# Swapping the operands of k'v in a TensorE-heavy attention and mixing kernel, and packing head pairs in column halves

## The chip, the cores and the metric

The kernel runs on one core of a Trainium2 chip. The metric is the device time in microseconds (us) from the start to the end of one execution; the kernel before was run three times. A profile of one execution stands beside the times. Its span is a little shorter than the time, as it counts from the first to the last recorded instruction.

The engines are TensorE (PE in the profile, its weight loads PEld), VectorE (DVE), ScalarE (ACT), GpSimd (POOL) and SyncE (SP), which here issues the DMAs.

## What is computed

Two blocks follow each other. The first is an attention whose score is a product of two sketches, and so linear in the sequence; the second mixes tokens with a phase (batch 4, heads 4, sequence 1088, head dimension 32, sketch size r = 8, model width 128). Cut to what matters:

```python
def phi(x):
    a = np.einsum('rd,bhsd->bhsr', S1, x)
    b = np.einsum('rd,bhsd->bhsr', S2, x)
    return np.einsum('bhsi,bhsj->bhsij', a, b).reshape(*x.shape[:-1], r * r)
q_p, k_p = (phi(q), phi(k))
kv = np.einsum('bhsf,bhsd->bhfd', k_p, v)         # <- the part that changes
z = np.sum(k_p, axis=2)
num = np.einsum('bhsf,bhfd->bhsd', q_p, kv)
den = np.einsum('bhsf,bhf->bhs', q_p, z)[..., None] + 1e-06
attn = num / den                                   # then (B, S, H*D) = x
theta = x @ w_theta
zr, zi = x * np.cos(theta), x * np.sin(theta)
y = np.einsum('ts,bsd->btd', w_tok_r, zr) + np.einsum('ts,bsd->btd', w_tok_i, zi)
u = x + y
out = u + np.maximum(u @ w_ch, 0.0)
```

`kv` is, for each batch and head, a 64 x 32 matrix: 64 features of a key times 32 values, summed over the sequence. The sequence lies in nine chunks of 128 rows on the partitions.

## The kernel before

The weights come as 64-bit floating point and are turned into fp32 on the chip. For w_tok, which is 34 pieces of 128 x 544, that takes three ScalarE and two VectorE instructions for each piece:

```python
def load_f32(dst, src):
    st = buf("st", [P, PIECE], I64, ST)[:p, :n]
    DMA.dma_start(st, src)
    lo, hi = split(st)
    step = buf("step", [P, NC * P], I16, 3)[:p, :2 * n].rearrange("p (n t) -> p n t", t=2)
    x = dst.bitcast(I32)
    A.activation(dst, hi.bitcast(F32), AF.Copy, scale=2.0**-112)
    A.activation(step[:, :, 1].bitcast(F16), hi.bitcast(F32), AF.Copy, scale=2.0**-60)
    A.activation(step[:, :, 0], lo.bitcast(U32), AF.Copy, scale=2.0**-29)
    ts(x, x, 3, ALU.logical_shift_left)
    tt(V, x, x, step..., ALU.add)
```

For each batch there are stages, named `keys`, `values`, `queries`, `mixed` and `mixing`:

- **keys**: load q, k, v; powers of two to scale by; the sums over keys from which the denominator comes (`ksl`, `cm`, `cz`, `tz`, `nz`, `mv`).
- **values**: transpose k (`big` to `fT`), multiply by the sketches (`s_bd`) to get `ks`, then the features `feat` (VectorE, 128 x 768 for three chunks) and their product with v, accumulated over the nine chunks in one PSUM tile `kv`, and copied into the block-diagonal `kvbd`.
- **queries**: slices of q (`qsl`), their products with `mv` (`lv`), the denominators (`fl`, `dgr`, `dn`, `rd`).
- **mixed**: features of the queries, transposed (`feat` to `fT`), times `kvbd` (`num`); x, its transpose `xT`, theta, cosine and sine; `zr`, `zi` and the last 64 rows of both in `z2`.
- **mixing**: 17 double rows of w_tok (`wT`) against z, in three groups of up to 384 tokens, then the last product with w_ch and the output.

The stage of the values that the change touches, as it was:

```python
    def keys_values(b):
        vn = tiles["v", b]
        kv = psum()[:, :4 * D].rearrange("p (n d) -> p n d", n=2)
        for g in range(NG):                      # 3 groups of 3 chunks
            ks = tiles["kf", b, g]
            kp = buf("feat", [P, CH, R, R], F32, 2)
            tt(V, kp, ks[:, :, 0:R]..., ks[:, :, R:2 * R]..., ALU.mult)
            for i in range(GC):
                for n in range(2):               # two pairs of heads
                    c = g * GC + i
                    T.matmul(
                        kv[:, n], kp[:, i * H + 2 * n:i * H + 2 * n + 2]...,   # weights: 128 columns
                        vn[:, c, 2 * n:2 * n + 2]...,                          # moving: 64 columns
                        start=(c == 0 and n == 0), stop=(c == NC - 1), skip_group_check=True)
        for j in range(2):
            pj = slice(j * R * R, (j + 1) * R * R)
            A.copy(kvbd[b % 2][pj, :, j * D:(j + 1) * D], kv[pj, :, j * D:(j + 1) * D])
```

A pair of heads has 2 x 64 = 128 features and 2 x 32 = 64 values. Of its 128 x 64 product only the two blocks on the diagonal are wanted.

The instructions are not issued in the order of the program text. Every operation is noted first, with a duration by rule and a due time; `lay_out` then places them on each engine: of the operations that could start soonest, the one with the earliest due time. This order is fixed when the kernel is built. The due times follow backward from those of the mixing matmuls, which start at `START[b]`, and are moved by `SOONER` for each stage:

```python
    def dues(self):
        for op in reversed(self.ops):
            for n in op.behind:
                other = self.ops[n]
                other.due = min(other.due, op.due - op.cost - other.late)
        for op in self.ops:
            op.due -= SOONER.get(op.stage, 0)
...
    order.due = START[b] + (PACE * n if len(gs) > 1 else 0.65 * (g * NK + n))
    T.matmul(yp[:, :t1 - t0], z, wT[:, i, t0:t1], start=(n == 0), stop=(n == NK - 1))
```

As all operations are issued from one helper, all have the line L320 in the profile; they are told apart by their tiles.

Of the kernel before, what the change touches and what calls it, by code (L numbers as in the profile page):

```python
# [32 lines left out]
P = 128  # L33
# [3 lines left out]
ROUND = 1.5 * 2.0**23  # L37
TWO_PI = 6.2831850
TINY = 2.0**-60
START = 90, 130, 170, 215  # L40
BIG = 5

SOONER = {"keys1": 20, "keys3": 15, "mixed0": 10, "mixed1": -5, "mixed2": 20, "mixed3": 15,
          "mixing0": -25, "mixing1": -35, "mixing2": -25, "mixing3": -10, "queries0": -5,
          "queries1": -5, "queries2": -10, "queries3": 5, "values0": -5, "values1": 20,
          "values2": 35, "values3": 40}
ST = 6
PACE = 2.5
PIECE = 544
# [64 lines left out]
class Order:  # L114
# [35 lines left out]
    def duration(self, engine, call, out, ins):  # L150

        n = math.prod(out.shape[1:])
        psum = any(isinstance(x, View) and x.buf.tag == "w" for x in ins)
        if engine == "DVE":
            if call == "tensor_reduce":
                n = math.prod(ins[0].shape[1:])
            if call == "reciprocal":
                return 0.29, 0.1
            own = any(isinstance(x, View) and x.shape[1:] == (1,) for x in ins[1:])
            fast = call in ("tensor_scalar", "tensor_copy", "memset") and not psum  # L160
            return 0.09 + n / (1920 if fast and not own else 1400 if fast else 970), 0.1
        if engine == "ACT":
            wide = any(isinstance(x, View) and x.buf.tag == "st" for x in ins)
            own = any(isinstance(x, View) and x.shape[1:] == (1,) for x in ins[1:])
            return 0.05 + 0.07 * own + n / (900 if out.dtype != F32 and wide else 1020 if wide else 1130), 0.15
        if engine == "SP":
            return 0.36, 0.0
        if call == "transpose":
            return 0.11, 0.3
        if ins[0].dtype == F32:  # L170
            return max(0.22, n / 600), 0.3
        return max(0.06, n / 2400), 0.3

    def note(self, engine, fn, call, a, kw):
# [30 lines left out]
    def dues(self):  # L205
# [4 lines left out]
        for op in self.ops:  # L210
            op.due -= SOONER.get(op.stage, 0)

# [111 lines left out]
def kernel(  # L324
# [12 lines left out]
    B, _, NC, H, D = q.shape  # L337
# [14 lines left out]
    V, A, T, DMA = order.dve, order.act, order.pe, order.sp  # L352

    def buf(tag, shape, dt=F32, bufs=1):
        return order.buffer(sb, tag, shape, dt, bufs)

    def psum():
        return order.buffer(ps, "w", [P, 512], F32, 8)

    def tt(eng, o, a, b, op):  # L360
        eng.tensor_tensor(out=o, in0=a, in1=b, op=op)
# [72 lines left out]
    ident = buf("ident", [P, P], F32)  # L434
# [16 lines left out]
    t_ = psum()  # L451
    T.transpose(t_[:2 * H, :P], View(hm.buf, hm.buf.slots[0]), ident)
    A.activation(hmT, t_[:2 * H, :P], AF.Copy, scale=512.0)
    hmTq = buf("hmTq", [P, P])[:H]
    t_ = psum()
    T.transpose(t_[:H, :P], hm, ident)
    A.activation(hmTq, t_[:H, :P], AF.Copy, scale=512.0)
# [81 lines left out]
    kvbd = []  # L539
    for b in range(2):  # L540
        t = buf(f"kvbd{b}", [P, 2, 2 * D], F32)
# [137 lines left out]
    def keys_values(b):  # L679

        vn = tiles["v", b]
        kv = psum()[:, :4 * D].rearrange("p (n d) -> p n d", n=2)
        for g in range(NG):
            ks = tiles["kf", b, g]
            kp = buf("feat", [P, CH, R, R], F32, 2)
            tt(V, kp, ks[:, :, 0:R].unsqueeze(3).to_broadcast([P, CH, R, R]),
               ks[:, :, R:2 * R].unsqueeze(2).to_broadcast([P, CH, R, R]), ALU.mult)
            for i in range(GC):
                for n in range(2):
                    c = g * GC + i  # L690
                    T.matmul(
                        kv[:, n], kp[:, i * H + 2 * n:i * H + 2 * n + 2].rearrange("p h i j -> p (h i j)"),
                        vn[:, c, 2 * n:2 * n + 2].rearrange("p h d -> p (h d)"),
                        start=(c == 0 and n == 0), stop=(c == NC - 1), skip_group_check=True)
        for j in range(2):
            pj = slice(j * R * R, (j + 1) * R * R)
            A.copy(kvbd[b % 2][pj, :, j * D:(j + 1) * D], kv[pj, :, j * D:(j + 1) * D])


    NT = NC * HR  # L700
# [145 lines left out]
    def mix_sums(b, gs, yps):  # L846
        zr, zi, zl = tiles["z", b]
        for n, i in enumerate(rows):
            z = zr[:, i] if i < NF else zi[:, i - NF] if i < NK - 1 else zl
            for g, yp in zip(gs, yps):  # L850
                t0, t1 = g * GC * P, min((g + 1) * GC * P, S)
                order.due = START[b] + (PACE * n if len(gs) > 1 else 0.65 * (g * NK + n))
                T.matmul(yp[:, :t1 - t0], z, wT[:, i, t0:t1], start=(n == 0), stop=(n == NK - 1))
# [40 lines left out]
    n = 2 * R  # L894
# [29 lines left out]
    for i in range(NL):  # L924
        T.matmul(pp[:, i * D:], s2x[:, i].rearrange("p h d -> p (h d)"), s2z[:, 0:NL - i],
                         start=(i == 0), stop=(i == NL - 1), skip_group_check=True)
# [21 lines left out]
    for b in range(B):  # L948
        if b:
            order.stage = f"keys{b}"  # L950
            load(b, "kqv")
            powers_of(b)
            order.stage = f"keys{b}"
            keys_slices(b)
        matrices(b)
        order.stage = f"values{b}"
        keys_features(b)
        keys_values(b)
        order.stage = f"queries{b}"
        query_slices(b)  # L960
        features(b)
        denominators(b, 0, NC)
        order.stage = f"mixed{b}"
        for g in range(NG):
            mixed(b, g, numerator(b, g))
        if b == 0:
            order.stage = "weights"
            for i in rows:
                for n in range(0, S, PIECE):
                    load_f32(wT[:, i, n:n + PIECE], w_tok[i][:, n:n + PIECE])  # L970
        order.stage = f"mixing{b}"
        mixing(b)
# [44 lines left out]
```

## Time and profile before

| | before |
|---|---|
| time, median of 3 | 297.95 us (297.94 to 299.46) |
| span of the profile | 296.2 us |
| TensorE busy, instructions recorded | 257.5 us (87%), 1347 |
| TensorE weight loads busy | 185.4 us (63%) |
| VectorE busy | 225.9 us (76%) |
| ScalarE busy | 165.3 us (56%) |
| mean granted TensorE clock | 0.928 |
| matmuls of the mixing stage (128 x 384 and 128 x 320) | 132.5 us in 384 records |
| matmuls of k'v | 19.3 us in 144 records |

A busy share is an average over the whole span. What an operation is worth depends on the stage in which it lies, so the shares are read slice by slice and not as totals. An fp32 matmul leaves two records, each with a weight load of its own. The length of a record is not what it costs when others follow at once: for that, take the distance from one start to the next.

### The profile page before, as it was taken

The numbers are of one execution on the slowest core, as the hardware profiler recorded it, in microseconds if no ns is written. First come the engines' busy times: TensorE is split into PE (matmuls) and PEld (weight loads), VectorE is DVE, ScalarE is ACT, GpSimd is POOL, SyncE is SP. The second block draws the span as 40 slices with busy tenths as digits, with TensorE's granted clock in tenths as the row PEclk, the third lists the DMA queues.
The fourth block names the chain that finished last, engine by engine and source line by source line (L and its number), as shares of the span: only waits on it lengthen the run. The fifth ranks groups of instructions, "written<-read, shape, count | busy, mean of one in ns | idle before, by whom it ended". The sixth has DMA issues, their size and how long they took to land.

```text
span 296.2 us, 4006 instructions
## 1 busy us (share of the span) xinstructions
PE 257.5 (87%) x1347; PEld 185.4 (63%) x1347; DVE 225.9 (76%) x646; ACT 165.3 (56%) x334; POOL 0.7 (0%) x6
## 2 busy tenths in 40 slices
PE   4569558837989999489999999999999999999993
PEld 3447437636966666257876676687758766665671
DVE  4999999999869999999998878999699561001011
ACT  3695559895299999999947225037914360000000
POOL 0000000000000000000000000000000000000000
PEclk9958859995599999979999999999999999999998
DMA  7970559671023757764000000000100000000001
GB/s 258 412 298 2 180 185 321 200 212 52 2 75 85 244 207 240 257 195 143 0 1 2 0 27 27 3 1 14 36 27 2 0 22 27 2 27 22 27 0 49
DMA packets 11603, 28.77 MB, mean 97 GB/s; under 512 B 1216, under 2 KB 5568, under 8 KB 11584
## 3 DMA queue, kind: packets, MB, share of 16 engines
q1 hardware_dynamic: 11584, 28.53, 28.7%
q8 instruction: 10, 0.16, 0.2%
q14 instruction: 9, 0.07, 0.1%
HBM read 26.30 MB, written 2.23 MB: 96 GB/s over the span
## 4 chain that ended last, share of the span: by engine, by line
PE 69%; DVE 15%; ACT 11%; DMA 3%; issue 1%; ACTq 0%; DVEq 0%
PE w L320 69%; ACT step L320 5%; DVE big L320 2%; DVE feat L320 2%; DVE lv L320 2%; DMA st<-w_tok 2%; DVE wT L320 1%; ACT wT L320 1%; ACT big L320 1%; DMA big<-k_l 1%; ACT lv L320 1%; DVE ksl L320 1%; DVE cut_r L320 1%; DVE m L320 1%; DVE fl L320 1%
## 5 line engine op out<-in xcount | busy, mean ns | idle before, releaser
L320 PE MATMUL w<-wT,st 128*128 128x384 f32 (+1 forms) x384 | 132.5, 476 | 1.9 <-DVE st L320 1.3
L320 PEld LDWEIGHTS w<-wT,st 128*128 128x128 f32 x384 | 67.7, 191 | 34.9 <-DVE st L320 2.2
L320 ACT ACTIVATE step<-st 128x544 f16<-128x544 f32 (+2 forms) x70 | 53.1, 808 | 1.8 <-DVE wT L320 1.7
L320 ACT COPY fT<-w 128x256 f32<-128x256 f32 (+1 forms) x48 | 18.5, 399 | 33.1 <-PE w L320 31.4
L320 ACT COPY ot<-w 128x384 f32<-128x384 f32 (+2 forms) x16 | 6.0, 395 | 47.8 <-PE w L320 47.7
L320 PE MATMUL w<-ident,feat 128*128 128x128 f32 x72 | 17.4, 311 | 9.5 <-ACT fT L320 6.1
L320 DVE SCALAR_TENSOR_TENSOR uT<-w,uT 128x384 f32<-128x384 f32 (+1 forms) x12 | 6.4, 532 | 25.2 <-PE w L320 25.1
L320 PEld LDWEIGHTS w<-kvbd,fT 128*128 128x128 f32 x144 | 23.5, 226 | 3.0 <-ACT fT L320 0.9
L320 DVE CUSTOM_DVE_ANT_0 wT<-wT,step 128x1088 uint16<-128x1088 uint16 x34 | 23.8, 717 | 0.3 <-ACT step L320 0.3
L320 PE MATMUL w<-kvbd,fT 128*128 128x64 f32 x144 | 24.0, 296 | 0.0
L320 PE MATMUL w<-big,feat 128*128 128x64 f32 x144 | 19.3, 276 | 5.0 <-DVE feat L320 5.0
L320 ACT ACTIVATE wT<-st 128x544 f32<-128x544 f32 x34 | 22.9, 696 | 1.0 <-DMA st<-w_tok 1.0
L320 PEld LDWEIGHTS w<-big,feat 128*128 128x128 f32 x144 | 18.2, 194 | 7.5 <-DVE feat L320 6.3
L320 PEld LDWEIGHTS w<-ident,feat 128*128 128x128 f32 x72 | 11.6, 179 | 12.0 <-ACT fT L320 7.1
L320 PE MATMUL w<-mv,qsl 128*128 128x192 f16 (+2 forms) x108 | 17.4, 286 | 1.8 <-DVE mv L320 1.6
L320 DVE TENSOR_TENSOR uT<-xT,w 128x384 f32<-128x384 f32 (+1 forms) x12 | 6.3, 528 | 16.2 <-PE w L320 16.2
L320 ACT COPY lv<-w 128x384 f32<-128x384 f32 x36 | 16.0, 483 | 3.7 <-PE w L320 3.7
L320 PE MATMUL w<-ident,big 128*128 128x128 f32 x72 | 13.9, 333 | 3.1 <-DMA big<-k_l 3.1
L320 PE MATMUL w<-s_bd,fT 128*128 128x64 f32 x72 | 11.8, 313 | 5.4 <-DVE pw L320 3.9
L320 PEld LDWEIGHTS <-qsl 128*128 128x128 f16 x108 | 10.6, 102 | 8.4 <-issue 4.2
L320 PE MATMUL w<-ksl 128*128 128x384 f16 x72 | 14.9, 360 | 0.9 <-ACT big L320 0.9
L320 PEld LDWEIGHTS w<-s_bd,fT 128*128 128x128 f32 x72 | 10.6, 223 | 6.6 <-DVE pw L320 4.2
(187 smaller groups left out, 412.7 us busy)
## 6 DMA issues: line engine op xcount, KB each, us to landing
st<-w_tok SPq DMA_DIRECT2D x34, 544.0 KB, 4.6
big<-k_l SPq DMA_DIRECT2D x4, 576.0 KB, 4.0
big<-q_l SPq DMA_DIRECT2D x4, 576.0 KB, 3.9
big<-v_l SPq DMA_DIRECT2D x4, 576.0 KB, 5.2
out<-ot SPq DMA_DIRECT2D x8, 192.0 KB, 2.1
out<-ot SPq DMA_DIRECT2D x4, 128.0 KB, 1.8
st<-w_sq SPq DMA_DIRECT2D x1, 256.0 KB, 3.8
out<-ot SPq DMA_DIRECT2D x4, 32.0 KB, 1.8
```

Source lines behind the costliest of these rows:

```text
L320: op.call(*r, **{k: x.real() if isinstance(x, View) else x for k, x in op.kw.items()})
```

## The change

The values become the weights and the features the moving operand: 64 weight columns in place of 128, 128 moving columns in place of 64. The product is then transposed (64 values by 128 features), and each of the two pairs of heads gets a half of TensorE's columns and of PSUM's partitions (`tile_position=(0, 0)` and `(0, 64)`), so that the two could run beside each other. At the end of each batch ScalarE copies the sum to SBUF, TensorE transposes it, and the copies into `kvbd` read the transposed tile. The rule for durations halves the cost of a matmul with at most 64 weight columns, and the due times of the stages are set anew. A small buffer (`hmTq`) shares the place of the new one.

```diff
--- before.py
+++ after.py
@@ -37,13 +37,13 @@
 ROUND = 1.5 * 2.0**23
 TWO_PI = 6.2831850
 TINY = 2.0**-60
-START = 90, 130, 170, 215
+START = 95, 130, 170, 215
 BIG = 5
 
-SOONER = {"keys1": 20, "keys3": 15, "mixed0": 10, "mixed1": -5, "mixed2": 20, "mixed3": 15,
-          "mixing0": -25, "mixing1": -35, "mixing2": -25, "mixing3": -10, "queries0": -5,
-          "queries1": -5, "queries2": -10, "queries3": 5, "values0": -5, "values1": 20,
-          "values2": 35, "values3": 40}
+SOONER = {"keys1": 20, "keys3": 10, "mixed0": 10, "mixed1": 15, "mixed2": 20, "mixing0": -25,
+          "mixing1": -35, "mixing2": -15, "mixing3": -10, "queries0": -25, "queries1": -5,
+          "queries2": -10, "queries3": -5, "values0": -5, "values1": 10, "values2": 15,
+          "values3": 35}
 ST = 6
 PACE = 2.5
 PIECE = 544
@@ -168,7 +168,7 @@
         if call == "transpose":
             return 0.11, 0.3
         if ins[0].dtype == F32:
-            return max(0.22, n / 600), 0.3
+            return max(0.22, n / 600) / (1 if ins[0].shape[1] > 64 else 2), 0.3
         return max(0.06, n / 2400), 0.3
 
     def note(self, engine, fn, call, a, kw):
@@ -451,7 +451,7 @@
     t_ = psum()
     T.transpose(t_[:2 * H, :P], View(hm.buf, hm.buf.slots[0]), ident)
     A.activation(hmT, t_[:2 * H, :P], AF.Copy, scale=512.0)
-    hmTq = buf("hmTq", [P, P])[:H]
+    hmTq = buf("kvt", [P, P])[:H]
     t_ = psum()
     T.transpose(t_[:H, :P], hm, ident)
     A.activation(hmTq, t_[:H, :P], AF.Copy, scale=512.0)
@@ -679,7 +679,7 @@
     def keys_values(b):
 
         vn = tiles["v", b]
-        kv = psum()[:, :4 * D].rearrange("p (n d) -> p n d", n=2)
+        kv = psum()[:, :P]
         for g in range(NG):
             ks = tiles["kf", b, g]
             kp = buf("feat", [P, CH, R, R], F32, 2)
@@ -688,13 +688,18 @@
             for i in range(GC):
                 for n in range(2):
                     c = g * GC + i
-                    T.matmul(
-                        kv[:, n], kp[:, i * H + 2 * n:i * H + 2 * n + 2].rearrange("p h i j -> p (h i j)"),
-                        vn[:, c, 2 * n:2 * n + 2].rearrange("p h d -> p (h d)"),
-                        start=(c == 0 and n == 0), stop=(c == NC - 1), skip_group_check=True)
+
+                    T.matmul(kv[n * 2 * D:(n + 1) * 2 * D], vn[:, c, 2 * n:2 * n + 2].rearrange("p h d -> p (h d)"),
+                             kp[:, i * H + 2 * n:i * H + 2 * n + 2].rearrange("p h i j -> p (h i j)"),
+                             start=(c == 0), stop=(c == NC - 1), tile_position=(0, n * 2 * D), skip_group_check=True)
+        kvt = buf("kvt", [P, P])
+        A.copy(kvt, kv)
+        t = psum()[:, :P]
+        T.transpose(t, kvt, ident)
+        t = t.rearrange("p (n d) -> p n d", n=2)
         for j in range(2):
             pj = slice(j * R * R, (j + 1) * R * R)
-            A.copy(kvbd[b % 2][pj, :, j * D:(j + 1) * D], kv[pj, :, j * D:(j + 1) * D])
+            A.copy(kvbd[b % 2][pj, :, j * D:(j + 1) * D], t[pj, :, j * D:(j + 1) * D])
 
 
     NT = NC * HR
```

## Prediction

> **What bounds the kernel now.** I read the page first, its forty slices before its totals, then the busy time by stretch, then the order of time on TensorE. In the slices (one is 7.4 us) the question is which row is full at the same time as which stage.
>
> ```profile
> PE   4569558837989999489999999999999999999993
> DVE  4999999999869999999998878999699561001011
> ACT  3695559895299999999947225037914360000000
> PEclk9958859995599999979999999999999999999998
> ```
>
> VectorE is full from slice 2 to slice 21, TensorE from slice 18 to the end, ScalarE in between, and TensorE's clock is low now and then before slice 12. So there are two stages: a first one that VectorE and ScalarE set (they turn the 17 double rows of w_tok into fp32 beside the work of batches 0 and 1), and a second one that only TensorE sets. To place the border I asked for the end of the w_tok conversion on VectorE, and for busy times on either side of it (columns: stretch, length, then busy us of PE, PEld, DVE, ACT, POOL).
>
> ```profile
> 146.13 0.72 DVE L320 CUSTOM_DVE_ANT_0 wT<-wT,step 128x1088 uint16<-128x1088 uint16 x1
> ...
> 0.00:60.00 60.00, 40.55 (x260) 31.62 (x260) 54.84 (x215) 41.22 (x81) 0.70 (x6) 0.83 0.64 234
> 60.00:90.00 30.00, 22.26 (x125) 19.93 (x126) 26.27 (x82) 21.18 (x47) 0.00 (x0) 0.72 0.26 76
> 90.00:130.00 40.00, 34.71 (x166) 23.25 (x165) 39.56 (x70) 39.06 (x71) 0.00 (x0) 0.96 0.65 214
> 130.00:146.10 16.10, 14.95 (x90) 10.86 (x90) 15.84 (x33) 15.47 (x30) 0.00 (x0) 0.99 0.31 98
> 146.10:296.20 150.10, 145.07 (x711) 99.77 (x709) 89.43 (x250) 48.35 (x111) 0.00 (x0) 0.99 0.06 16
> ```
>
> Up to 146.1 us VectorE is busy for 54.84 + 26.27 + 39.56 + 15.84 = 136.5 us, so only 9.6 us of it are idle; TensorE is idle for 146.1 - 112.5 = 33.6 us. After it TensorE works for 145.07 of 150.10 us, and most of the missing 5 us is the last output's way. The chain of waits agrees: from 138.4 to 289.9 us it is TensorE alone. A saving on TensorE counts in full in the second stage and hardly at all in the first.
>
> What the operation itself costs I read from the order of time on TensorE (start, length, tiles, number of records).
>
> ```profile
> 157.93 1.45 PE L320 MATMUL w<-big,feat 128*128 128x64 f32 x12
> 159.21 5.38 PE L320 MATMUL w<-wT,st 128*128 128x384 f32 x16
> 164.43 0.24 PE L320 MATMUL w<-tz,pbd 128*128 128x32 f16 x4
> ```
>
> Every fp32 matmul leaves two records: k'v is 4 batches x 9 chunks x 2 pairs = 72 instructions, and the page counts 144. Twelve records of k'v from 157.93 to 159.21 are 107 ns each; sixteen mixing records from 159.21 to 164.43 are 326 ns each, 0.85 ns a column. At that rate 64 moving columns would be 54 ns, so k'v does not wait for its moving operand. [...]
>
> ```profile
> L320 PE MATMUL w<-big,feat 128*128 128x64 f32 x144 | 19.3, 276 | 5.0 <-DVE feat L320 5.0
> L320 PEld LDWEIGHTS w<-big,feat 128*128 128x128 f32 x144 | 18.2, 194 | 7.5 <-DVE feat L320 6.3
> ```
>
> A record is 276 ns long but starts every 107 ns; the difference, some 170 ns, is pipeline that the next one hides.
>
> [...]
>
> **The change part by part.** *The matmuls.* Swapped, a record has 64 weight columns[...] and 128 moving columns. A 128 x 128 fp32 transpose, with as many moving columns, starts every 110 ns in this trace. So the swap alone gains nothing: 107 becomes 110. All depends on the second half of the columns running beside the first; then two records take 110 ns, 55 each. All 144: 144 x 107 = 15.4 us becomes 7.9, a saving of 7.5. By stages: batches 0 and 1 have their k'v before 60 us and batch 2 between 108 and 126, where TensorE has gaps; only batch 3 (36 records from 157.9 to 172.9) is in the second stage: 36 x 52 = 1.9 us.
>
> *What is added.* A ScalarE copy of 128 x 128 (about 0.3 us by the one activation of that shape) and a transpose (two records, 0.22 us) for each batch, and one more hop ahead of kvbd. In the second stage: 0.2 us of TensorE. I chose to leave the longer hop out, since other TensorE work fills it there.
>
> *Mode changes.* By the order of the changed kernel the 72 instructions stand in 5, 10, 4 and 4 runs for batches 0 to 3, other matmuls between them. Each run is entered and left: 46 changes, 8 of them in the second stage. At no more than 0.17 us that is up to 1.4 us there, so the matmuls by themselves are worth 1.9 - 0.2 - (0 to 1.4) = 0.3 to 1.7 us at the end.
>
> *The due times.* These move more. I laid both orders beside each other and took as the border the first mixing matmul of batch 0's last row, which needs the last w_tok row. Behind it the changed kernel has 18 k'v instead of 18 (1.9 us less), 6 fewer of each of the num, x-transpose and theta matmuls (18 x 0.217 = 3.9 us less), 2 fewer wide mixing ones (1.3), three small ones fewer (0.2) and three other transposes or so more (0.5): some 6.6 us of TensorE less by such rates, 147.0 against 153.6. Before, the 153.6 took 296.2 - 146.3 = 149.9 us, a ratio of 0.976, so the changed second stage should take 147.0 x 0.976 = 143.5 us.
> That work has not vanished; it is ahead of the border, and there VectorE pays. Up to and with its last w_tok conversion its instructions sum by the mean durations of their rows to 171.7 us against 164.6. Means overlap (all its rows sum to 267.6, the page has 225.9 busy), so 7.1 becomes 7.1 x 0.844 = 6.0 us more. If VectorE keeps its 9.6 us of idle time, the border moves from 146.3 to 152.3 and the end to 295.8 us. If half the idle time goes (batch 1 is begun sooner, which gives VectorE something to do where it had waited), the border is at 147.5. The dues were set anew for the new order, so I take two thirds of the way between the two, 149.1, which is a choice and no measurement. With 143.5 us behind it and 0.8 us for mode changes the profile ends at 293.4 us. The measured time is 297.95 - 296.2 = 1.75 us more than the span: **295.1 us**.
>
> **The rivals.** (A) The halves do not overlap. Then k'v stays at 110 ns a record, the second stage is 1.9 us longer and the mode changes are pure loss: 297 to 298.5. [...] I give this 30%. (B) The border just moves: VectorE's extra 6.0 us delay the last w_tok row and eat the shorter second stage; about 297.5. For it: VectorE at 39.56 of 40 us from 90 to 130. (C) The retuned dues also remove the low clock between 60 and 90 us (0.72) and VectorE's gaps, so the border stays at 147 to 148: 147.5 + 143.5 + 1.75 = 292.7, and below 292 if the tail has no mode cost. [...]
>
> **Range and chances.** The end is the sum of two numbers that I know to about 2 us each: the border (147 to 153) and the rest (142 to 146). That gives 290.5 to 298.5 us. 2% faster is below 292.0, which needs (C) together with overlapping halves: 0.17. 2% slower is above 303.9; nothing above gets there save a wait in the second stage that I don't see: 0.03.
>
> **What would show it.** In the changed profile: the k'v records under the reversed names, 144 of them, with starts 55 ns apart inside a run (right) or 110 (rival A); a gap of 0.1 to 0.2 us at either end of a run (mode change) or none; four transposes of kvt; the last w_tok conversion on VectorE near 150 us (147 for C, 152 for B); TensorE full behind it and about 143 us long. If TensorE shows idle time behind the border that waits for kvbd or feat, the prediction is wrong for a reason not listed; if the end moves by more than 2% with the border and the rest both as before, the reading of two stages is wrong.

## The result and the profile after

The changed kernel takes **303.19 us** (median; 303.04 to 303.81) beside 298.22 us for the kernel before on the same chip: a ratio of 1.016, with a 95% interval of 1.013 to 1.020. Ratios, here and below, leave out executions more than 1.5% above the shortest of the same kernel, which the medians keep. It is slower by 5 us. The prediction was 295.1 us with a range up to 298.5, so it was wrong. The span of the profile is 301.1 us (before 296.2), the mean granted TensorE clock 0.905 (0.928).

The forty slices of the changed kernel, one 7.5 us:

```profile
PE   4659592870598889999999999999999999999993
DVE  5998979979996999999999966998851995600011
ACT  4693559799963999888973225327614135500000
PEclk9959867596555899999999999999999999999998
```

Counted from 1, TensorE has a hole in slices 10 and 11 (0 and 5), where the kernel before has 7 and 9 and a smaller hole of its own in slice 9 (3); the clock is low in slices 11 to 13; and from slice 16 on TensorE is full, where it was full to the end only from slice 19 before. Next the busy time by stretch (columns: stretch, length, busy us of PE, PEld, DVE, ACT and POOL, then the clock, the DMA share and GB/s). The first two stretches end and begin at the border, the first mixing matmul of batch 0's last row; the last one is the stretch before the border in which TensorE has no gap:

```profile
0.00:155.90 155.90, 119.29 (x678) 86.59 (x678) 141.50 (x416) 123.07 (x240) 0.70 (x6) 0.82 0.48 170
155.90:301.10 145.20, 140.21 (x676) 93.17 (x674) 85.37 (x231) 43.80 (x98) 0.00 (x0) 0.99 0.06 16
70.00:80.00 10.00, 1.19 (x6) 1.06 (x6) 10.00 (x17) 10.00 (x18) 0.00 (x0) 0.50 0.54 200
80.00:90.00 10.00, 10.00 (x48) 9.07 (x47) 9.62 (x29) 7.06 (x17) 0.00 (x0) 0.50 0.66 228
90.00:100.00 10.00, 8.88 (x37) 6.47 (x38) 7.10 (x28) 4.80 (x11) 0.00 (x0) 0.50 0.25 82
...
107.00:156.00 49.00, 49.00 (x269) 34.18 (x268) 47.20 (x97) 46.13 (x91) 0.00 (x0) 1.00 0.38 127
```

The same view of the kernel before, for the stretches that differ most:

```profile
70.00:80.00 10.00, 9.68 (x49) 9.04 (x49) 8.97 (x29) 3.12 (x8) 0.00 (x0) 0.50 0.01 2
80.00:90.00 10.00, 8.66 (x53) 7.17 (x52) 7.62 (x27) 9.15 (x19) 0.00 (x0) 0.87 0.19 57
90.00:100.00 10.00, 10.00 (x44) 6.29 (x43) 10.00 (x14) 10.00 (x18) 0.00 (x0) 1.00 0.50 155
...
107.00:156.00 49.00, 42.56 (x238) 30.82 (x238) 48.33 (x104) 42.39 (x79) 0.00 (x0) 0.97 0.44 147
```

The border in the order of time on TensorE, before and after:

```profile
146.31 0.81 PE L320 MATMUL w<-wT,z 128*128 128x384 f32 x2
```

```profile
155.86 0.86 PE L320 MATMUL w<-wT,z 128*128 128x384 f32 x2
```

It went from 146.3 to 155.9 us (+9.6), and what lies behind it from 149.9 to 145.2 us (-4.7). That is the whole of the +4.9 us. Ahead of the border VectorE is busy for 141.5 us (136.7 before) and idle for 14.4 (9.6).

TensorE's side tells more. I cut the span into stretches of 2 us and split each in three: idle (length less busy), lost to the low clock (busy times one less the clock), and the rest, work at full clock. The split is an estimate from two spacings: twelve `num` records from 85.33 to 87.94 us take 218 ns each at clock 0.50, and eight in the kernel before, from 147.31 to 148.23, take 115 ns each at 1.00.

| TensorE, us | idle | lost to low clock | work at full clock | span |
|---|---|---|---|---|
| before, to 108 us | 27.2 | 13.7 | 67.1 | |
| before, behind it | 11.5 | 1.6 | 175.2 | 296.2 |
| after, to 108 us | 36.6 | 18.3 | 53.0 | |
| after, behind it | 5.0 | 0.0 | 188.2 | 301.1 |

At 108 us the changed kernel is 14.1 us of TensorE work behind (9.4 more idle, 4.6 more at low clock). It wins back 8.1 us because TensorE has no more gaps afterwards, and 1.1 us because its work is less; some 4.9 us stay. Over the whole span that is 2.9 us more idle time, 3.0 us more at low clock and 1.1 us less work. What a us at low clock is worth can't be read from this pair alone: the profile of the kernel before is one of its executions with a high mean clock (0.928), most have 0.904 to 0.917, and on one chip 297.93 us at 0.928 stands beside 297.95 us at 0.908.

Where the 14 us went is seen in the order of time on TensorE (start, length, tiles, records, and in brackets the idle time before it and who ended it):

```profile
61.16 0.34 PE L320 MATMUL w<-mv,qsl 128*128 128x384 f16 x1
61.42 0.43 PE L320 MATMUL w<-feat,big 128*64 128x128 f32 x2
61.79 0.30 PE L320 MATMUL w<-mv,qsl 128*128 128x288 f16 x1
...
65.05 0.55 PE L320 MATMUL w<-ident,big 128*128 128x128 f32 x3
78.81 1.30 PE L320 MATMUL w<-ident,feat 128*128 128x128 f32 x5 [13.21 <-DVE feat L320]
```

TensorE waits 13.2 us for the first features of batch 0's queries (5.6 before, from 62.7 to 68.3, where ScalarE's copy `fT` came last). VectorE, ahead of these features:

```profile
67.91 0.72 DVE L320 CUSTOM_DVE_ANT_0 wT<-wT,step 128x1088 uint16<-128x1088 uint16 x1
...
69.21 0.71 DVE L320 CUSTOM_DVE_ANT_0 wT<-wT,step 128x1088 uint16<-128x1088 uint16 x1
...
74.62 1.35 DVE L320 CUSTOM_DVE_ANT_0 wT<-wT,step 128x1088 uint16<-128x1088 uint16 x2
...
77.72 1.82 DVE L320 TENSOR_TENSOR feat<-fl 128x768 f32<-128x768 f32 x2
```

The new due times put w_tok pieces (six last conversions from 60 to 78 us; the kernel before has none between 60.4 and 80) in front of the features, which begin at 77.7 us instead of 67.2. Of these 10.5 us, 5.7 are there already when `fl`, from which they are made, begins (66.94 instead of 61.22). The rest comes between `fl` and the features: some 3.3 us of w_tok pieces, and some 2 us of slicing (`step` and `big`) that the kernel before has behind its features. ScalarE is as full there: 10.00 of 10 us from 70 to 80. After the wait TensorE has clock 0.50 until 100 us, through ten us in which it is busy without a gap (10.00 of 10 from 80 to 90).

### The profile page after: what moved, and what is told of

It reads as the page before. It is cut to its first block, busy times and chain, and to the rows that moved or that the text cites. A ratio compares the mean times of both kernels' runs of the same rounds, so it can differ in the third digit from the quotient of the medians.

```text
span 301.1 us, 4002 instructions
## 1 busy us (share of the span) xinstructions
PE 259.5 (86%) x1351; PEld 179.8 (60%) x1351; DVE 226.9 (75%) x646; ACT 166.9 (55%) x338; POOL 0.7 (0%) x6
## 4 chain that ended last, share of the span: by engine, by line
PE 78%; DVE 13%; ACT 3%; DMA 3%; issue 2%; ACTq 0%; DVEq 0%
PE w L320 78%; DMA big<-k_l 3%; DVE big L320 2%; DVE wT L320 2%; ACT step L320 1%; DVE m L320 1%; DVE cut_r L320 1%; ACT big L320 1%; DVE feat L320 1%; DVE fl L320 1%; DVE cut_z L320 1%; ACT lv L320 0%; DVE mx L320 0%; DVE ksl L320 0%; DVE lv L320 0%
## 5 line engine op out<-in xcount | busy, mean ns | idle before, releaser
L320 PE MATMUL w<-wT,st 128*128 128x384 f32 (+1 forms) x384 | 130.9, 473 | 0.0
L320 ACT COPY fT<-w 128x256 f32<-128x256 f32 (+1 forms) x48 | 18.3, 397 | 25.9 <-PE w L320 22.4
L320 PE MATMUL w<-mv,qsl 128*128 128x192 f16 (+2 forms) x108 | 21.9, 324 | 8.2 <-DVE mv L320 6.0
L320 PE MATMUL w<-ident,feat 128*128 128x128 f32 x72 | 15.3, 312 | 13.2 <-DVE feat L320 13.2
L320 ACT COPY lv<-w 128x384 f32<-128x384 f32 x36 | 16.7, 485 | 17.3 <-PE w L320 17.0
L320 PE MATMUL w<-s_bd,fT 128*128 128x64 f32 x72 | 13.3, 318 | 4.8 <-DVE pw L320 4.4
L320 PEld LDWEIGHTS w<-s_bd,fT 128*128 128x128 f32 x72 | 11.3, 224 | 6.9 <-DVE pw L320 4.6
L320 PE MATMUL w<-feat,big 128*64 128x128 f32 x144 | 15.4, 295 | 0.0
L320 DVE TENSOR_SCALAR wT<-wT 128x544 int32<-128x544 int32 x34 | 14.4, 432 | 0.0
L320 PEld LDWEIGHTS w<-ident,big 128*128 128x128 f32 x72 | 11.1, 178 | 4.7 <-DMA big<-k_l 3.2
```

Source lines behind the costliest of these rows:

```text
L320: op.call(*r, **{k: x.real() if isinstance(x, View) else x for k, x in op.kw.items()})
```

## The experiments

Most kernels here keep the **order of one kernel on every engine** and change only what is issued at a place in it. Four that were laid out anew told little, as will be seen; they stand behind those with filler. Each ratio is to the kernel before on the same chip, with its 95% interval.

**New order, old k'v.** Laid out as the changed kernel; in the places of k'v the old form is issued, and the transpose is left out.

```diff
-  T.matmul(kv[half n], vn[..n..], kp[..n..], tile_position=(0, n * 2 * D), ...)
-  A.copy(kvt, kv); T.transpose(t, kvt, ident); A.copy(kvbd.., t..) twice
+  nc.tensor.matmul(kvo[:, n], kp[..n..], vn[..n..], ...)   # same places in the order
+  nc.scalar.copy(kvbd.., kvo..) twice                      # in the place of the first copy
```

> The changed kernel's order of instructions on every engine, kept as it is, but k'v in its old form (128 weight columns, no copy and transpose at the end). Theory D (the new due times lose the time: batch 0's query features come at 77.7 us in place of 67.2, TensorE waits 13.2 us for them and is at half clock from 70 to 100 us; the swapped k'v itself is worth 0 to 2 us): 303 to 306 us, no better than the changed kernel. Rival K (the swapped k'v itself is slow, by mode changes and the longer hop to kvbd): 297 to 300 us.

Measured 303.58 us, ratio 1.016 (1.012 to 1.019); border 156.2, rest 145.6. The wait for the query features is there too:

```profile
77.69 1.30 PE L323 MATMUL w<-ident,feat 128*128 128x128 f32 x5 [12.77 <-ACT step L323]
```

So **the order of the changed kernel, which its due times and durations make, loses the 5 us by itself**; the new form of k'v in it is worth 0.4 us, which the intervals don't tell from nothing.

**Old order, new k'v.** The reverse: the order of the kernel before, the new form in the places of the old, the transpose three TensorE instructions later.

```diff
-  T.matmul(kv[:, n], kp[..n..], vn[..n..], ...)
+  nc.tensor.matmul(kvn[half n], vn[..n..], kp[..n..], tile_position=(0, n * 2 * D), ...)
+  nc.scalar.copy(kvt, kvn); transpose after 3 more TensorE operations; copies after 1 more of ScalarE
```

> The order of the kernel before, kept as it is, but k'v in its new form in two column halves, with the copy, the transpose (a few TensorE instructions later) and the copies into kvbd. Theory D: 296 to 298.5 us, at or a little below the kernel before. Rival K: 301 to 304 us, most of the loss is there.

301.30 us, 1.009 (1.006 to 1.013); border 149.0, rest 150.6. The new form costs about 2.6 us in the old order, so there rival K is right. Two differences show in the trace, neither tested by itself. The stretch in which mv and k'v of batches 0 and 1 alternate takes 8.4 us (53.30 to 61.68) instead of 6.5 (52.95 to 59.41); but the granted clock was 0.64 from 54 to 56 us and 0.51 from 56 to 58, where it was 1.00 before, and that alone is 1.7 us of work by the split used above (2.00 x 0.36 + 2.00 x 0.49). And kvbd of batch 3 now ends a wait of 0.5 us on TensorE at 177 us.

**Both pairs in one half.** The changed kernel; both pairs use the first 64 columns and partitions.

```diff
-  kv[n * 2 * D:(n + 1) * 2 * D] ... tile_position=(0, n * 2 * D)
+  kvo[:, n]                                                     # kvo: 64 partitions, 2 x 128
```

> The changed kernel's order, operands swapped, but both pairs of heads in the first half of the columns (PSUM partitions 0 to 63, one pair behind the other), then two half copies by ScalarE in place of one. If the halves run beside each other in the changed kernel (its k'v records start 67 ns apart in a run): 107 to 112 ns here, and 1 to 3 us longer than the changed kernel, 304 to 306 us. If they do not: 67 ns here as well and 303 us. If the column tiles cost by mode changes more than they bring: below 303 us.

308.82 us, 1.032 (1.027 to 1.037), longer than the forecast. The order of time on TensorE, this kernel and then the changed one:

```profile
170.94 1.52 PE L702 MATMUL w<-feat,big 128*64 128x128 f32 x12
172.40 0.91 PE L323 MATMUL w<-uT,w 128*128 128x384 f32 x2
```

```profile
28.96 0.88 PE L320 MATMUL w<-feat,big 128*64 128x128 f32 x12
29.77 0.43 PE L320 MATMUL w<-s_bd,fT 128*128 128x64 f32 x2
```

Twelve records in one half take 1.46 us from start to start, 122 ns each; in two halves 0.81 us, **67 ns**. So the halves do overlap, 1.8 times and not twice.

**Grouped, new order.** The changed kernel's order; the six k'v instructions of a group are held until the last is due and issued together, which leaves 12 runs.

```diff
+  op.emit = hold(op) until 2 * GC are held, then issue all six
```

> The changed kernel's order, the six k'v instructions of a group of chunks together at the place of the last. Mode changes as the cost: batch 1's ten runs become three, 1 to 2 us less ahead of the first query features: 301.5 to 302.8 us. VectorE's own chain sets that stage: 303 to 303.5 us.

301.76 us, 1.010 (1.006 to 1.013): 1.4 us less than the changed kernel. Work at full clock falls from 241.2 to 237.1 us, idle time grows from 41.6 to 42.9. Standing alone so cost the k'v instructions 4 us of TensorE and, by the medians, 1.4 of the time; the intervals of the two kernels still touch.

**Grouped, old order.** The same in the order of the kernel before.

> As the run with the order of the kernel before and k'v in its new form, but the six k'v instructions of a group of chunks stand together at the place of the last of them: 12 runs or fewer in place of one run for each place where other matmuls came between. If the changes of tiling are what the new form costs there (about 0.25 us for an instruction that stands alone, about 10 of them ahead of the border): the border comes back from 149.0 to 147 us or less and the time is 298 to 299.5 us, as the kernel before. If the changes cost nothing and the longer hop to kvbd does: 301 to 301.5 us as ungrouped.

301.80 us, 1.011 (1.007 to 1.015); border 148.4. That is close to the second forecast, though the changes of tiling do cost something: the query features are back at 67.3 us and work at full clock falls from 242.3 to 238.4. In this pair of profiles 5.8 us more go to the low clock (21.1 against 15.3). The twelve theta records of this kernel, then of the kernel before:

```profile
82.92 2.18 PE L335 MATMUL w<-w,xT 128*128 128x128 f32 x12
84.94 0.27 PE L335 MATMUL w<-ident,feat 128*128 128x128 f32 x1
```

```profile
82.73 1.56 PE L320 MATMUL w<-w,xT 128*128 128x128 f32 x12
84.12 0.27 PE L320 MATMUL w<-ident,feat 128*128 128x128 f32 x1
```

The same work takes 2.02 us instead of 1.39 there; the clock was 0.50 from 82 to 84 us and 0.94 from 84 to 86, where the kernel before had 0.84 and 1.00.

**Filler in the wait, new order.** The changed kernel with 28 dummy fp32 matmuls of 128 x 256 in the 13 us wait.

```diff
+  for _ in range(28): nc.tensor.matmul(tr[:, :2 * P], ident, w2, ...)   # ahead of batch 0's first query transpose
```

> The changed kernel with 28 more fp32 matmuls of 128x256 (about 12 us at full clock), whose output is written over, ahead of batch 0's first query transpose, where TensorE waited 13.2 us. They keep TensorE busy through the wait. Theory: the low clock behind the wait is what costs (18 us of TensorE work at half speed from 80 to 100 us, with VectorE waiting for it 3 to 5 us): clock near 1.0 from 80 us on and 297 to 300 us. Rival: VectorE alone sets the stage, and the clock costs nothing: 302.5 to 304 us.

302.12 us, 1.011 (1.007 to 1.016); border 153.9. TensorE is busy for 12.00 of 12 us from 66 to 78, at clock 1.00. By stretch:

```profile
70.00:80.00 10.00, 8.92 (x44) 7.38 (x42) 10.00 (x19) 10.00 (x16) 0.00 (x0) 1.00 0.51 192
80.00:90.00 10.00, 7.49 (x51) 6.43 (x51) 9.94 (x29) 7.72 (x19) 0.00 (x0) 0.87 0.68 236
90.00:100.00 10.00, 8.24 (x42) 5.32 (x42) 8.93 (x33) 6.28 (x14) 0.00 (x0) 0.67 0.31 93
```

The clock is up, though not wholly (0.67 from 90 to 100). What is lost to it ahead of 108 us falls from 18.3 to 13.9 us, as in the kernel before (13.7). The border comes 2.0 us sooner, the time 1.1, and both forecasts missed. By this run most of the loss is not the clock's; the last run with filler, below, leaves a doubt.

**Filler elsewhere.** Five more kernels ask what the clock costs in the other orders, and in the new order with k'v grouped. Two of them put the filler (12 matmuls) into the PSUM buffer of the first query transpose:

> The kernel before with 12 more fp32 matmuls of 128x256 (about 5.2 us), whose output is written over, in the 5.6 us in which TensorE waits for the first query features. Theory that the low clock behind that wait (0.50 from 70 to 80 us) costs here as it did in the changed kernel (where filling gave 1.1 us): clock 0.9 or more from 70 to 80 us and 296 to 297.8 us, below the kernel before. If the clock is free here because VectorE is full: 298 to 299 us.

> Grouped k'v in its new form in the order of the kernel before, and the 12 filling matmuls as well. If the effects add: the grouped run's time less what filling gives the kernel before, so 295.5 to 298 us, below both kernels. If the new form has no gain in the second stage either: as the filled kernel before or a little above.

300.79 us (1.009, 1.005 to 1.013) and 305.16 us (1.019, 1.013 to 1.025): the filler stood behind that buffer and so the transpose came only at 74.3 and 76.1 us. They test nothing but that. The next two wrote to columns of an earlier buffer that nobody reads (24 matmuls of 128 x 128):

> The kernel before with 24 more fp32 matmuls of 128x128 (5.2 us) in the 5.6 us wait for the first query features, this time into unused columns of a PSUM buffer that nobody reads before 130 us, so they start at once. Clock theory: first query transpose at 68.3 us as before, clock 0.9 to 1.0 from 70 to 80 us in place of 0.50, TensorE's work of 68 to 87 us done some 5 us sooner, and VectorE's waits of 0.8 and 2.0 us behind it gone: 295.5 to 297.5 us. If VectorE's instructions alone set that stage: 298 to 299 us.

> Old order, k'v in its new form and grouped, and the same 24 matmuls in the same wait. If the 3 us that the grouped run lost to the kernel before were lost clock: level with the filled kernel before or up to 1 us below it, 295 to 297.5 us. If they are the longer hop to kvbd and VectorE: 2 to 3 us above the filled kernel before.

The kernel before with it: 298.18 us, ratio 0.9998 (0.998 to 1.002). Grouped k'v in the old order with it: 300.97 us, 1.009 (1.006 to 1.012), border 148.2 and rest 151.0 against 147.2 and 150.0. From 70 to 80 us the clock was 0.64 in the first (0.50 without filler, forecast 0.9 to 1.0) and 0.78 in the second (0.50 in the grouped run without filler). So the part of the low clock that the filler took away, 1.9 us of work in the first (9.68 x 0.50 less 8.13 x 0.36), is worth nothing in the kernel before; the whole was not tested. In the old order the new k'v still loses its 2.8 us with less low clock.

> The changed kernel's order with k'v grouped and the 28 filling matmuls in its 13.2 us wait. Each alone took 1.1 and 1.4 us off the changed kernel's 303.2. If they add: 300 to 301.2 us, still above the kernel before, since VectorE's 4.8 us of work moved ahead of the last w_tok row remain. If only one of them can act: 301.5 to 302.2 us.

Grouped k'v and the 28 filler matmuls in the new order: 301.76 us, 1.005 (1.001 to 1.008). By the median of twenty executions that is no less than grouping alone, and the border in the profile is at 154.8 us in both. The lower ratio says little, since it counts only the shortest seven of the twenty. But two of these took 297.13 and 298.61 us, and they are the two with the highest mean clock, 0.948 and 0.946; the others have 0.917 to 0.931. The profile is of one of the others: there the filler held the clock only from 70 to 80 us (1.00) and not from 80 to 90 (0.55). So in this order a clock that stays up may be worth 3 to 4.6 us, nearly the whole loss. That is two executions without a trace, and no test.

**Laid out anew.** Four kernels change due times or the form of k'v and let the order follow.

```diff
 e1: the changed kernel with START and SOONER of the kernel before
 e2: the kernel before with START and SOONER of the changed kernel
 e4: the changed kernel,  -"queries0": -25  +"queries0": -5
 e7: the kernel before,   +"weights": 5
```

> The changed kernel with START and SOONER as in the kernel before; the order is laid out anew. Border theory (the end is VectorE's work up to the last w_tok conversion, plus its idle time, plus TensorE's work behind): by the orders VectorE has 137.9 us before the border and TensorE 146.1 us behind it (149.7 x 0.976), so a span of 284.1 + 7 to 13 us of idle time = 291 to 297 and a time of 293 to 299 us. Theory that the swapped k'v costs some 2.6 us wherever it stands: 300 to 302 us.

> The kernel before with START and SOONER of the changed one; the order is laid out anew. Border theory: VectorE 138.2 us before the border, TensorE 155.5 behind it, so a span of 293.7 + 7 to 13 = 301 to 307 and a time of 302 to 308 us: the new due times lose with the old k'v too. Rival (the loss comes only with both together): 297 to 300 us.

> The changed kernel with one due time as before: batch 0's queries 20 us sooner (queries0 -5 in place of -25); the order is laid out anew. Border theory: VectorE 142.7 us before the border, TensorE 144.8 behind it: 287.5, and with idle time as in the kernel before (7 us) to as in the changed one (13 us) a span of 294.5 to 300.5 and a time of 296 to 302 us; TensorE's wait for the first query features should shrink from 13.2 us to under 6 us. If the late queries of batch 0 are not the cause: 303 us and the long wait stays.

> The kernel before with the w_tok stage due 5 us sooner than its dates said; the order is laid out anew. The last conversion then has only 108.0 us of VectorE's work ahead of it and TensorE 170.7 us behind its border: 278.7 + 7 to 13 = 286 to 292 and a time of 288 to 294 us, if the end is still VectorE's part plus TensorE's part. If batch 0's z and not w_tok holds TensorE then, TensorE waits behind the border and it is 298 us or more.

308.94 (1.035, 1.033 to 1.038), 307.33 (1.028, 1.025 to 1.032), 307.46 (1.027, 1.020 to 1.034) and 352.38 us (1.180, 1.177 to 1.184); e2 came as expected. In e7 the second forecast did (298 us or more, with TensorE waiting behind the border: 12.7 of the first 50.2 us there are idle, though the longest waits are for `feat` and `cz` and not for z). e1 and e4 met neither of theirs; in e4 the wait for the first query features shrank only from 13.2 to 10.9 us, and its four executions lie between 304.40 and 312.22. Due times are not terms of a sum: one number of the table moves the whole order. In e7, where the w_tok stage is due 5 us sooner, TensorE keeps clock 0.51 from 60 to 110 us and the rest is 201.7 us long. The table also shows what the new due times are for: with the old ones the swapped k'v costs 10.6 us (308.94 against 298.36), with the new ones 5; and either form of k'v with the table of the other comes to 307 to 309.

**VectorE's work taken away.** Three kernels (h1, h2 and h3, in this order) leave out the two VectorE instructions (0.42 + 0.72 us) of five w_tok pieces, 5.7 us in all, so those pieces are not those of the reference; the order is kept.

```diff
+  if seen[m] - 1 in LEAVE: continue      # shift and add of the 7th to 11th piece (h1), 22nd to 26th (h2, h3)
```

> The order of the changed kernel, kept; the two VectorE instructions of five w_tok pieces (the 7th to 11th in VectorE's order, between 60 and 76 us) are left out, so these pieces of w_tok are not those of the reference. That is 5 x 1.14 = 5.7 us less VectorE ahead of batch 0's first query features, which were ready at 77.7 us. If the time is lost because TensorE stands still behind VectorE at 65 to 79 us, its wait of 13.2 us shrinks by 3 to 5.7 us, the border comes from 155.9 to 150.5 to 153 and the time from 303.2 to 297.5 to 300.5. If ScalarE (10.0 of 10 us busy from 70 to 80) or the clock sets it all the same: the wait stays above 11 us, time 302 to 303.5.

302.44 us, 1.010 (1.005 to 1.016); span 300.4, border 155.4. TensorE's order of time:

```profile
76.56 1.30 PE L327 MATMUL w<-ident,feat 128*128 128x128 f32 x5 [10.69 <-DVE feat L327]
...
78.97 0.19 PE L327 MATMUL w<-tz,pbd 128*128 128x32 f16 x1 [1.10 <-ACT ks L327]
79.61 1.54 PE L327 MATMUL w<-kvbd,fT 128*128 128x64 f32 x6 [0.46 <-ACT fT L327]
```

The features come 2.25 us sooner (75.47 on VectorE), but two waits on ScalarE (1.6 us) take their place, ScalarE being busy for 10.00 us from 70 to 80 as before; 0.5 us reach the border. So neither forecast came whole: the wait shrank by 2.5 us, to below 11, and the time is that of the second one.

> The order of the changed kernel, kept; the same two VectorE instructions are left out for five pieces of w_tok that stand between 115 and 137 us, so these pieces are not those of the reference. Again 5.7 us less VectorE ahead of the border. If VectorE's work sets the border, as the prediction had it, the border comes from 155.9 to 150 to 151.5 and the time from 303.2 to 298 to 299. If TensorE, which has no gap from 107 us on, sets the border by its own queue, the border stays at 155 or later and the time at 302.3 to 303.5.

302.59 us, 1.011 (1.006 to 1.016); span 301.4, border 156.2. One stretch of it:

```profile
107.00:156.00 49.00, 48.86 (x267) 33.98 (x267) 43.34 (x87) 46.53 (x92) 0.00 (x0) 1.00 0.38 127
```

VectorE has 3.9 us less work there than in the changed kernel, TensorE is full all the same, and the border has not moved forward. **In the changed kernel VectorE's work does not set the border; TensorE's own queue does.**

> The order of the kernel before, kept; the two VectorE instructions of five w_tok pieces that stand between 113 and 127 us are left out, so these pieces are not those of the reference. If VectorE's work sets the border there, as the prediction read it, the border comes from 146.3 to 140.5 to 142.5 and the time from 298.2 to 292.5 to 294.5. If TensorE's own queue sets it there too, only the few waits of TensorE on VectorE between 107 and 138 us go (1.3 us by the order of time), and the time is 296.5 to 298.5.

298.70 us, ratio 1.001 (0.998 to 1.004). The stretch ahead of the border in this kernel, and in the kernel before:

```profile
107.00:146.00 39.00, 32.94 (x172) 23.58 (x171) 33.77 (x60) 36.87 (x67) 0.00 (x0) 0.87 0.55 186
```

```profile
107.00:146.00 39.00, 32.56 (x179) 23.44 (x179) 38.71 (x72) 37.42 (x68) 0.00 (x0) 0.96 0.55 184
```

The border is at 147.5 us (146.3 in the kernel before), so five us less of VectorE bring nothing even there. Two things stand beside it: ScalarE is as full (37 of 39 us) as VectorE had been, and the clock was lower in this profile, 0.87 against 0.96, which is 3 us of work (32.94 x 0.13 less 32.56 x 0.04). The clock doesn't hide a gain in the times, though: the executions have mean clocks of 0.906 to 0.922, and those of the kernel before on that chip 0.900 to 0.927. What holds the border there I did not separate.

## Why the prediction was wrong, point by point

- **Halves overlap: right, the size off.** 67 ns a record, not 55, where transposes with as many moving columns take 110 and both pairs in one half 122; rival A was false. What sets the 107 ns of the old form, no run here separates.
- **Mode changes: right in size, and counted in the wrong place.** The mixing group of 16 behind a k'v run takes 5.32 us in the old order with the new k'v (161.51 to 166.83), where it took 5.22. These 0.10 us are within the 0.17 us of the prediction, which was an estimate: the 276 ns of a record less the 107 ns from start to start. But an instruction that stands alone between others takes 0.37 us (61.42 to 61.79 above), where the old form in the same order took 0.20, both at clock 1.00:

```profile
60.38 0.36 PE L702 MATMUL w<-big,feat 128*128 128x64 f32 x2
60.58 0.33 PE L323 MATMUL w<-mv,qsl 128*128 128x384 f16 x1
```

  Its gain is gone and more. Two records in one half are 0.24 us at the 122 ns measured there, so some 0.13 us (an estimate: 0.37 less 0.24) are left for the two changes. Grouping wins 4.1 us of TensorE work, 3.6 of it ahead of the border, where the prediction counted none.
- **The transpose: too dear.** It leaves one record (four `kvt` transposes, four records) that costs 0.11 us from start to start (184.54 to 184.65), not two. The six x-transposes in the prediction's sum are dear in the same way: that term is some 3.3 us and not 3.9.
- **The rest behind the border: right.** 144.3 predicted with the mode changes, 145.2 measured. The new form itself is 0.4 us of that (the rest is 145.6 with the old form in the same order), where 0.3 to 1.7 was predicted.
- **VectorE's added work ahead of it: right.** 6.0 us predicted, 4.8 measured.
- **The border: the step that failed.** The prediction took VectorE's work plus a share of its 9.6 us of idle time, "two thirds of the way between the two, 149.1, which is a choice and no measurement". Measured is 155.9. The idle time did not shrink to 6.4 us, it grew to 14.4. On TensorE the 9.6 us by which the border moved are about 3.5 us more work ahead of it, 3.0 us more at low clock and 3.0 us more idle time, by the split used above. Below the choice lies the model: that VectorE sets the first stage and that "a saving on TensorE counts in full in the second stage and hardly at all in the first". The prediction's own chain already had TensorE alone from 138.4 us, 8 us ahead of the border before. The runs showed otherwise: 5.7 us less VectorE moved the border by -0.5 us ahead of the wait and by +0.3 us behind 107 us. In the changed kernel TensorE is full for 49 us ahead of the border, so what it had lost until then, by waiting or at clock 0.50, is in the end. The range was also narrower than its terms: 153 + 146 + 1.75 is 300.75, not 298.5, and the measured time lies above that too.
- **What the added idle time is.** TensorE waits 7.6 us longer for the query features, with w_tok pieces and slicing ahead of them on VectorE and ScalarE both. That these pieces make the wait is read from the trace; taking VectorE's part of five away shortened it by 2.5 us and moved the border by 0.5. Clock 0.50 from 80 to 100 us follows; with the wait filled it was 0.87 and 0.67. Its share is 2.0 us of border by the filler, and perhaps more by the two short executions. VectorE then waits for TensorE, not the reverse, as in the changed kernel's order of time on VectorE:

```profile
91.60 0.28 DVE L320 TENSOR_REDUCE mx<-w 8x1 f32<-8x128 f32 x1 [1.95 <-PE w L320]
...
94.94 0.17 DVE L320 COPY pw<-w 128x9 f32<-128x9 f32 x1 [1.30 <-PE w L320]
```

- **The due times.** I took them as retuned, so as good for the new form as the old ones for the old. They are better than the old ones for it, and still 5 us behind the old kernel, in the order that they make whatever the form of k'v. Rival B (the border just moves) had the direction; rival C (no low clock left) was false: the clock is at 0.50 from 70 to 100 us, where it had been from 70 to 80.

**Open:** whether leaving out ScalarE's part of the early pieces as well would bring the features and the border forward (not tried); why grouped k'v in the old order keeps 2 to 3 us; how the 5 us divide between the long wait and the low clock behind it; and whether the gains of clock and grouping add. No version here beat the kernel before by its median beyond the noise.

## What to carry to other kernels

Before calling an engine free in a stage, sum its idle time and its time at low clock and ask whether the stretch that follows is full: if it is, what was lost earlier is in the end. Two engines that are full side by side are tested by taking work from one, not by adding up its busy time. And where a scheduler lays out the order, an operation and its due times are to be measured apart, with the order kept; changed together they hide each other. A share lost to a low clock is to be looked at over several executions: here one kernel kept its time with 0.02 less of mean clock.

## What was not expected of the hardware

- After the 13.2 us wait TensorE worked for 10.00 of 10 us from 80 to 90 us and still had clock 0.50 until 100 us; no run here shows why. In the kernel before a stretch of 9.68 of 10 us (70 to 80) was at 0.50 as well.
- Two column halves: 67 ns a record of k'v (64 weight columns, 128 moving columns, fp32) in a run, 122 ns in one half.
- A lone k'v instruction with 64 weight columns between others with 128: 0.37 us, some 0.17 us more than the old form, with 128, in such a place (0.20).
